# Units of up to 288 tokens with stationary weights, beside slots of 128 tokens, in the expert stage of an attention, FFN and MoE kernel

## The chip, the cores and the metric

The kernel runs on one core of a Trainium2 chip. The metric is the device time of one execution in microseconds (us). The median of three runs of the kernel before is 658.79 us (658.10 to 659.89).

## The reference

Three layers follow each other on 4 batches of 576 positions, 2304 tokens of 512 numbers. First comes attention with 8 heads of 64 and a window of 64 positions. Then a gated FFN: `h = relu(x @ w_in)`, a 3-tap convolution of h along the sequence, `(h * sigmoid(conv)) @ w_out`. The last layer is the one that the change touches. It sends each token to one of 8 experts:

```python
for s in range(S):
    fresh_e = argmax(logits[b, s])
    e = fresh_e if s == 0 or local_gate[b, s] < 0.5 else prev_e
    p = softmax(logits[b, s])
    h = np.maximum(x[b, s] @ w1[e], 0.0)      # 512 -> 1024
    out[b, s] = p[e] * (h @ w2[e])            # 1024 -> 512
```

With the reference's inputs (seed 0) the experts 0 to 7 get 336, 124, 567, 401, 257, 532, 13 and 74 tokens. The kernel does not know these numbers beforehand: it computes the routing on the chip.

## The kernel before

Attention and FFN run interleaved, batch by batch. In the last batch TensorE also computes the logits, and the routing follows while TensorE still makes the last FFN outputs (`tail`, line L484 with 512 columns, L524 with 256). Those outputs go to a scratch tensor `y_dram`, one row per token. The block `with tc.manual_schedule(engines=...)` at the end of the function fixes the order of TensorE (PE), VectorE (DVE) and ScalarE (ACT) by hand: `ahead(n)` emits the next n FFN matmuls, `next(sl)` the next part of `slots_of`, `cast` and `rest_of` prepare the first weights.

`slots_of` cuts each expert's tokens into slots of 128. It makes 0/1 matrices: `A` (the place of a token in its slot) and `bm` (which slot, which token). 18 matmuls of `A` with `bm` (L882) turn them into `gidx`, the row of `y_dram` for each place of each slot, and `sidx`, where its result goes; places that no token fills get a row that is not written. `eslot` is a slot's expert, `echg` says whether it differs from the slot before. A second product (L919) gives `pslot`, the probability by which a result is scaled. Slot 0 is not gathered whole: its rows come from a gather of `y_dram` (L1180, tile x0) and from the last two FFN tiles, through matmuls with `ident` and `aZ` (L514).

`run` then treats slots one by one; 23 of at most 25 are unrolled, the other two stand under `tc.If`. For a slot t:

- `gather(t)` (L1041): 128 rows of 2 KB from `y_dram` into SBUF, issued by GpSimd (POOL).
- `X(t)`: four transposes on PE into `psX`, then ACT copies the rounded part `xh` and DVE the remainder `xl`.
- `MM1`: 24 matmuls of 512 columns (three products of high and low parts, four blocks of 128 inputs, two halves of the 1024 hidden numbers). The tokens are the stationary operand, the weights move. ACT applies relu (L1074).
- `HT`: eight transposes of h (L1085), again split into `hh` (ACT, L1087) and `hl` (DVE, L1088).
- `MM2`: 24 matmuls of 512 columns (L1100), ACT scales the result (L1105), POOL scatters 128 rows (L1106).
- weights: `load1`/`load2` on SyncE's (SP's) queue into `raw1`/`raw2` (2 MB each, in four pieces, skipped where `echg` is 0); `split` makes high parts (ACT, L1017) and low parts (DVE, L1022). Every slot is split anew, also where the expert stays. There are two sets of split weights for each of w1 and w2.

All of a slot's steps stand in one fixed order per engine; MM2 of slot t-1 stands behind MM1 of slot t, so that ACT and DVE have a whole matmul phase to finish `hh` and `hl`.

## Time and profile before

| | |
|---|---|
| median of 3 runs | 658.79 us |
| profiled execution | 659.42 us, span 657.4 us |
| TensorE busy | 630.4 us (96%) |
| VectorE busy | 500.2 us (76%) |
| ScalarE busy | 468.2 us (71%) |
| GpSimd busy | 122.3 us (19%) |
| slots computed | 23 (23 scatters, L1106) |

The span is what the profiler sees between the first and the last instruction; the execution's own time is 2.0 us longer. TensorE's matmuls overlap in the records: one of 512 columns is shown with 0.39 us, while the next one starts 0.23 us after it. So the distance between starts is read, not the duration.

### The profile page before, as it was taken

What the parts mean: (1) busy time and instruction counts of PE and PEld (TensorE: products, weight loads), DVE (VectorE), ACT (ScalarE), POOL (GpSimd) and SP (SyncE); (2) the same over time, 40 slices, a digit from 0 to 9 for tenths busy, and PEclk for the clock granted to TensorE, in tenths of its full rate; (3) what the DMA queues carried; (4) which work ended last, traced back from release to release, by engine and by line L of the source; (5) the groups of instructions that cost most, each with busy time, mean ns of one, the idle gap of its engine ahead of it and who ended that gap; (6) DMA issues with size and microseconds to landing.
All of it is one profiled execution on the core that took longest, in us unless ns stands there. A gap on an engine that the chain in (4) does not pass through costs nothing.

```text
span 657.4 us, 12963 instructions
## 1 busy us (share of the span) xinstructions
PE 630.4 (96%) x4422; PEld 551.4 (84%) x4422; DVE 500.2 (76%) x995; ACT 468.2 (71%) x991; POOL 122.3 (19%) x158
## 2 busy tenths in 40 slices
PE   6879899999999999999999999999999999999995
PEld 5658898999999999999868778888888888888883
DVE  3789999426782388627766798998998988988982
ACT  3577688547792588735624688888888888888881
POOL 3412000001330023233602212112112112111101
PEclk9889999999999999999999999999999999999998
DMA  7894433332334211144001157504333434503770
GB/s 184 196 241 116 110 93 94 95 101 54 70 77 110 65 38 34 49 166 171 2 33 64 35 207 268 176 32 129 137 111 118 139 120 162 170 33 102 241 253 13
DMA packets 90885, 75.77 MB, mean 115 GB/s; under 512 B 71266, under 2 KB 71282, under 8 KB 90816
## 3 DMA queue, kind: packets, MB, share of 16 engines
q1 hardware_dynamic: 85696, 62.80, 32.3%
q0 software_dynamic: 3776, 10.80, 4.9%
q10 hardware_dynamic: 1344, 1.31, 0.7%
q8 instruction: 36, 0.59, 0.4%
q14 instruction: 33, 0.27, 0.1%
HBM read 127.84 MB, written 11.27 MB: 212 GB/s over the span
## 4 chain that ended last, share of the span: by engine, by line
PE 36%; issue 32%; DMA 14%; DVE 11%; ACT 4%; POOL 2%; POOLq 0%; ACTq 0%; DVEq 0%
PE psO L484 14%; PE psM L442 11%; DMA out_dram<-h,sidx 10%; PE psA L219 2%; DMA raw<-in_moe_w_in_dram 2%; PE psA L296 2%; POOL xg L1041 1%; DVE lf L570 1%; PE psA L271 1%; DVE sS L256 1%; PE psA L186 1%; ACT sS L243 1%; DVE lf L572 1%; PE psG L553 1%; DVE sS L231 1%
## 5 line engine op out<-in xcount | busy, mean ns | idle before, releaser
L442 PE MATMUL psM<-x,winH 128*128 128x288 f32 x512 | 109.3, 303 | 0.0
L442 PEld LDWEIGHTS psM<-x,winH 128*128 128x128 f32 x512 | 82.0, 188 | 1.0
L471 POOL TENSOR_TENSOR gL<-h,gH 128x64 fp32r<-128x64 f32 (+5 forms) x46 | 44.3, 975 | 204.5 <-ACT gH L470 102.3
L442 PE MATMUL psM<-x,winL 128*128 128x288 f32 x256 | 75.3, 295 | 0.0
L484 PE MATMUL psO<-woutH,gH 128*128 128x262 f32 (+2 forms) x240 | 68.3, 314 | 1.3 <-ACT gH L470 1.0
L1022 DVE TENSOR_TENSOR gL<-raw,gH 128x1024 fp32r<-128x1024 f32 x56 | 65.6, 1220 | 2.2 <-ACT gH L1017 0.7
L1106 POOL DMA_INDIRECT out_dram<-h,sidx x23 | 23.4, 1016 | 233.3 <-ACT h L1105 228.5
L484 PE MATMUL psO<-woutL,gH 128*128 128x262 f32 (+2 forms) x240 | 66.2, 303 | 0.0
L484 PE MATMUL psO<-woutH,gL 128*128 128x262 f32 (+2 forms) x240 | 64.8, 300 | 0.0
L243 ACT ACTIVATE sS<-sS,mx 128x128 f32<-128x128 f32 (+1 forms) x144 | 55.1, 387 | 7.7 <-DVE mx L231 7.7
L1022 DVE TENSOR_TENSOR winL<-raw,winH 128x1024 fp32r<-128x1024 f32 x48 | 56.4, 1235 | 3.6 <-ACT winH L1017 3.6
L1017 ACT ACTIVATE gH<-raw 128x1024 fp32r<-128x1024 f32 x56 | 55.8, 1066 | 0.0
L1022 DVE TENSOR_TENSOR woutL<-raw,woutH 128x1024 fp32r<-128x1024 f32 x44 | 51.0, 1221 | 2.8 <-ACT woutH L1017 2.8
L442 PEld LDWEIGHTS psM<-x,winL 128*128 128x128 f32 x256 | 48.0, 188 | 0.1
L1017 ACT ACTIVATE winH<-raw 128x1024 fp32r<-128x1024 f32 x48 | 47.0, 1061 | 0.0
L1100 PE MATMUL psO<-x,hh 128*128 128x512 f32 x144 | 46.7, 404 | 0.0
L1022 DVE TENSOR_TENSOR x<-raw,x 128x1024 fp32r<-128x1024 f32 x36 | 42.0, 1220 | 5.2 <-ACT x L1017 4.2
L484 PEld LDWEIGHTS psO<-woutH,gH 128*128 128x128 f32 x240 | 42.4, 189 | 3.9 <-ACT gH L470 1.4
L1100 PE MATMUL psO<-gH,hh 128*128 128x512 f32 x112 | 44.6, 398 | 0.0
L1100 PE MATMUL psO<-gH,hl 128*128 128x512 f32 x112 | 44.0, 393 | 0.0
L484 PEld LDWEIGHTS psO<-woutL,gH 128*128 128x128 f32 x240 | 42.7, 189 | 1.2
L1100 PE MATMUL psO<-gL,hh 128*128 128x512 f32 x112 | 43.7, 391 | 0.0
(289 smaller groups left out, 1625.8 us busy)
## 6 DMA issues: line engine op xcount, KB each, us to landing
raw<-in_moe_w_dram SPq DMA_DIRECT2D x184, 512.0 KB
v<-in_v_dram SPq DMA_DIRECT2D x56, 128.0 KB
y_dram<-ysb SPq DMA_DIRECT2D x18, 256.0 KB
kt<-in_k_dram SPq DMA_DIRECT2D x32, 128.0 KB
raw<-in_moe_w_out_dram SPq DMA_DIRECT2D x8, 512.0 KB
qt<-in_q_dram SPq DMA_DIRECT2D x30, 128.0 KB
raw<-in_moe_w_in_dram SPq DMA_DIRECT2D x6, 512.0 KB
raw<-in_moe_w_in_dram ACTq DMA_DIRECT2D x2, 512.0 KB
```

The lines of the kernel that those rows point to most:

```text
L186: nc.tensor.transpose(ps[:, n * P:(n + 1) * P], src[:, n].rearrange("p h d -> p (h d)"), ident)
L219: nc.tensor.matmul(ps[:, j * P + lo:(j + 1) * P], qbd[:, c, :], kT[:, k0:W * (c + 1)], start=True, stop=True)
L231: nc.vector.tensor_tensor_reduce(sS[:, c, lo:P], ps[:, j * P + lo:(j + 1) * P], mask[:, lo:P], -scale, -NEG, op0=ALU.add, op1=ALU.min, acc ...
L243: nc.scalar.activation(sS[:, c, lo:P], sS[:, c, lo:P], AF.Exp, scale=-1.0, bias=mx[:, c:c + 1], accum_out=sume[:, c:c + 1],)
L296: nc.tensor.matmul(ps[64 * h:64 * h + 64, W * (c - c0):W * (c - c0) + W], vt[:, h, :], a[:, c % 3, 64 * h:64 * h + 64], start=True, stop=True,
L442: nc.tensor.matmul(ps[:, 0:HS], wt[:, kk, f * P:(f + 1) * P], xt[:, c0:c0 + HS], start=n == 0, stop=n == 3 * KD - 1,)
L471: e1.tensor_tensor(gL[:, f, r:r + m], t[:, done:done + m], gH[:, f, r:r + m].bitcast(F32), op=ALU.subtract)
L484: nc.tensor.matmul(p_[:, 0:cs.stop - cs.start], gt[:, kk, r:r + P], wt[:, kk, cs], start=n == 0, stop=n == 3 * KF - 1,)
L1017: nc.scalar.activation(H_, raws[kk], AF.Copy)
L1022: nc.vector.tensor_tensor(L_, raws[kk], H_.bitcast(F32), op=ALU.subtract)
L1100: nc.tensor.matmul(ps, a[:, kk], w[:, kk % 2, :], start=n == 0, stop=n == 3 * KF - 1)
L1106: nc.gpsimd.indirect_dma_start(out=out[:, :], out_offset=bass.IndirectOffsetOnAxis(ap=sidx[:, t:t + 1].bitcast(U32), axis=0), in_=o, in_of ...
```

## The change

`units` is a fixed list: slots (S) and big units (B) alternate, S B S B S B S B S B S, and then more slots, up to 15 slots and 5 big units. 14 units, 9 S and 5 B, are always run; the other six slots stand in `If`s within each other. `slots_of` gets a planner: which experts give a big unit (up to 256 tokens and up to 32 of the next slot, at most 5 in all), how many slots stay, and which column of `gidx`, `sidx` and `pslot` each original slot becomes. The tables are made transposed (`tabI`, `tabP`), copied to SBUF by ACT and permuted by small matmuls (`placed`).

In a big unit the weights are stationary and up to 288 tokens move: `first_B` has 8 groups of 12 matmuls of 288 columns and needs no transposes of h; `second_B` has 4 groups of 24, and its output is transposed back by `Y` (12 transposes) during the slot that follows. `X` has 12 transposes for a big unit. MM2 now stands directly behind MM1 of its own unit; there is one set of split w2 in place of two, and one buffer of x and of gathered rows. The splits are handed out as jobs between matmul groups. Cut to its core:

```diff
+        NB = 5
+        XB = 32
+        WB = 2 * P + XB
         TS = (N + E * (P - 1)) // P
-        TB = TS - 2
+        NS = TS - 2 * NB
+        units = [("S", 0)]
+        for i in range(NB):
+            units += [("B", i), ("S", i + 1)]
+        units += [("S", i) for i in range(NB + 1, NS)]
+        NU = 2 * NB + 4
...
+            def table(m, name):
+                ps = pst(m * TS, P)
+                for i in range(NT):
+                    nc.tensor.matmul(ps, bm[:, i, 0:m].rearrange("p c t -> p (c t)"), rt["A"][:, i, :], start=i == 0, stop=i == NT - 1)
+                nc.scalar.activation(rt[name][:, 0:P], ps, AF.Copy)
+                return rt[name]
+
+            ti = table(2, "tabI")
...
+            def placed(t, c):
+                n = t.shape[0]
+                ps = pst(P, NCOL)
+                nc.tensor.matmul(ps[:, 0:CX], t[:, 0:P], perm[0:n, c], start=True, stop=True)
+                for j in range(3):
+                    nc.tensor.matmul(ps[:, CX:NCOL], t[:, j * XB:j * XB + P], permx[0:n, c, j], start=j == 0, stop=j == 2)
+                return ps
+
+            ps_i = placed(ti, 0)
+            v.tensor_scalar(gidx, ps_i, -float(P), 0.0, op0=ALU.add, op1=ALU.max)
...
+    def X(t):
+        xh, xl = xT_
+        for j, (_, u, n) in enumerate(cols(t)):
+            ps = psx() if j < 2 else psy().rearrange("p (k x) -> p k x", x=P)
+            for kk in range(KD):
+                nc.tensor.transpose(ps[:, kk, 0:n], xg[j][0:n, kk * P:(kk + 1) * P], ident[0:n, 0:n])
+            nc.scalar.activation(xh[:, :, u:u + n], ps[:, :, 0:n], AF.Copy)
+            nc.vector.tensor_tensor(xl[:, :, u:u + n], ps[:, :, 0:n], xh[:, :, u:u + n].bitcast(F32), op=ALU.subtract)
...
+    def Y(t, j):
+
+        c, u, n = cols(t)[j]
+        ps = psy()
+        for d in range(KD):
+            nc.tensor.transpose(ps[0:n, d * P:(d + 1) * P], yT_v[:, d, u:u + n], ident)
+        nc.scalar.activation(o_v[j][0:n], ps[0:n], AF.Copy, scale=pslot[0:n, c:c + 1])
+        scatter(c, n, o_v[j])
...
+    def first_B(t, after):
...
+        for f in range(KF):
+            ps = ps_h.tile([P, DM], F32, tag="h", name="psH")[:, 0:WB]
+            n = 0
+            for kk in range(KD):
+                H_, L_ = (w[:, f * P:(f + 1) * P] for w in ws[kk])
+                xh, xl = x[kk]
+                for a, w in ((H_, xh), (H_, xl), (L_, xh)):
+                    nc.tensor.matmul(ps, a, w, start=n == 0, stop=n == 3 * KD - 1)
+                    n += 1
+            nc.scalar.activation(hh[:, f], ps, AF.Relu)
+            nc.vector.scalar_tensor_tensor(hl[:, f], ps, 0.0, hh[:, f].bitcast(F32), op0=ALU.max, op1=ALU.subtract)
+            after(f)
...
+        def ahead():
+            if not end:
+                X(t + 1)
+                if t + 2 < NU:
+                    gather(t + 2)
+
+        if kind == "S":
+            y = [lambda j=j: Y(t - 1, j) for j in range(3)] if before else [lambda: None] * 3
+            job(2)
+            first_S(t, {
+                (0, 6): (y[0], job), (0, 10): (y[1],),
+                (1, 4): (job, lambda: HT(0),), (1, 6): (y[2],), (1, 10): (lambda: job(9),),
+            })
+            ahead()
+            jobs.extend(second)
+            second_S(t, {3: (lambda: HT(1), lambda: job(9))})
+        else:
+            first_B(t, lambda f: job())
+            job(9)
+            ahead()
+            jobs.extend(second)
+            second_B(t, lambda d: job(2))
+            job(9)
...
+            if t == 0:
+                step(t, (), w1_jobs(1))
+            elif units[t][0] == "B":
+                step(t, w1_jobs(t + 1) + w2_jobs(t), w1_jobs(t + 2))
+            else:
+                step(t, w2_jobs(t), w1_jobs(t + 2) if t > 2 * NB - 1 else ())
```

A job of `w1_jobs(t)` or `w2_jobs(t)` is one cast on ACT and one subtraction on DVE; the last of four also emits the load of the next unit's weights.

What stands on PE around the first routing product, in the kernel before (psR<-bm,A is the product, psO an FFN output):

```order
L484 MATMUL psO<-woutL,gH 128x512
L484 MATMUL psO<-woutH,gL 128x512
L484 MATMUL psO<-woutH,gH 128x512
L882 LDWEIGHTS A
L882 MATMUL psR<-bm,A 128x50
```

and in the kernel after, where the product is followed by 24 FFN matmuls and then by `placed` (L1011, L1013):

```order
L926 LDWEIGHTS bm
L926 MATMUL psR<-A,bm 50x128
L484 MATMUL psO<-woutH,gH 128x512
L484 MATMUL psO<-woutL,gH 128x512
L484 MATMUL psO<-woutH,gL 128x512
...
L1011 LDWEIGHTS tabI
L1011 MATMUL psR<-perm,tabI 128x25
L1013 LDWEIGHTS tabI
L1013 MATMUL psR<-permx,tabI 128x5
L484 MATMUL psO<-woutH,gH 128x512
```

The first product stands 16 FFN matmuls earlier than before, and PE has a second place at which it needs DVE's result (`perm`, `permx`).

What stands on ACT through a slot of the kernel before (casts of w2, relu of MM1, x of the next slot, casts of w1, the result):

```order
L1087 ACTIVATE hh<-psX 128x512 x2
L1017 ACTIVATE x<-raw_0_3859 128x1024
L1017 ACTIVATE x<-raw_1_3860 128x1024
L1017 ACTIVATE x<-raw_2_3861 128x1024
L1017 ACTIVATE gH<-raw_3_3862 128x1024
L1074 ACTIVATE h<-psH 128x512 x2
L1055 ACTIVATE xh<-psX 128x512
```

and through the first half of a slot behind a big unit of the kernel after (L1264 the outputs of `second_B`, L1126 casts, L1201 the results of `Y`, L1219 relu, L1192 `HT`):

```order
L1264 ACTIVATE h<-psO 128x288 x2
L1126 ACTIVATE x<-raw_0_3859 128x1024
L1126 ACTIVATE x<-raw_1_3860 128x1024
L1201 ACTIVATE o_4822<-psY,pslot 128x512
L1126 ACTIVATE x<-raw_2_3861 128x1024
L1201 ACTIVATE o_4823<-psY,pslot 128x512
L1219 ACTIVATE h<-psH 128x512
L1126 ACTIVATE gH<-raw_3_3862 128x1024
L1192 ACTIVATE gH<-psX 128x4x128
```

Before the first relu of the slot ACT now has the last output of the big unit, three casts and two results of `Y`; the transposes of h follow in the middle of the slot's own first phase.

DVE in a big unit of the kernel after takes turns between the low part of a group's relu (L1236) and that of a weight piece (L1130):

```order
L1236 SCALAR_TENSOR_TENSOR gL<-psH,gH 128x288
L1130 TENSOR_TENSOR winL<-raw_0_3855,winH 128x1024
L1236 SCALAR_TENSOR_TENSOR gL<-psH,gH 128x288
L1130 TENSOR_TENSOR winL<-raw_1_3856,winH 128x1024
L1236 SCALAR_TENSOR_TENSOR gL<-psH,gH 128x288
```

There was no such turn before: DVE split weights in blocks of four.

## Rows read from the trace of the kernel before

**Rows 1.** Busy time by stretch: us, then PE, PEld, DVE, ACT, POOL, PEclk, DMA share, GB/s
```profile
362.35:648.84 286.49, 286.24 (x1376) 234.60 (x1376) 253.05 (x248) 240.83 (x313) 47.31 (x44) 1.00 0.41 140
604.00:612.40 8.40, 8.40 (x44) 6.89 (x44) 7.64 (x9) 6.69 (x10) 2.04 (x2) 1.00 0.87 304
```

**Rows 2.** Timeline of POOL, first and last of 19 scatters: start us, us, what
```profile
407.79 1.02 POOL L1106 DMA_INDIRECT out_dram<-h,sidx  x1 [10.10 <-ACT h L1105]
...
631.53 1.00 POOL L1106 DMA_INDIRECT out_dram<-h,sidx  x1 [11.46 <-ACT h L1105]
```

**Rows 3.** Timeline of PE, from a slot's last matmul to the next slot
```profile
567.90 0.39 PE L1100 MATMUL psO<-gH,hl 128*128 128x512 f32 x1
568.13 1.03 PE L1085 MATMUL psX<-ident,h 128*128 128x128 f32 x8
568.92 0.48 PE L1070 MATMUL psH<-woutH,xh 128*128 128x512 f32 x1
```

**Rows 4.** Timeline of PE, 12 FFN matmuls of 288 columns: first, and next group
```profile
310.06 0.43 PE L442 MATMUL psM<-x,winH 128*128 128x288 f32 x2
...
311.65 0.45 PE L553 MATMUL psG<-gH,woutH 128*10 128x256 f32 x2
```

**Rows 5.** Groups by line, 290 to 330 us: count | busy us, mean ns | idle
```profile
L442 PEld LDWEIGHTS psM<-x,winH 128*128 128x128 f32 x113 | 18.2, 188 | 0.6
L449 ACT ACTIVATE h<-psM 128x288 f32<-128x288 f32 x16 | 6.4, 398 | 3.1 <-PE psM L442 3.1
```

**Rows 6.** Groups by line, expert stage
```profile
L1022 DVE TENSOR_TENSOR gL<-raw,gH 128x1024 fp32r<-128x1024 f32 x56 | 65.6, 1220 | 2.2 <-ACT gH L1017 0.7
L1017 ACT ACTIVATE gH<-raw 128x1024 fp32r<-128x1024 f32 x56 | 55.8, 1066 | 0.0
L1088 DVE TENSOR_TENSOR hl<-psX,hh 128x512 fp32r<-128x512 f32 x46 | 29.8, 686 | 12.3 <-ACT hh L1087 12.3
L1105 ACT ACTIVATE h<-psO,pslot 128x512 f32<-128x512 f32 x22 | 15.2, 692 | 27.0 <-issue 25.8 <-PE psO L1100 1.2
```

**Rows 7.** Timeline of DVE and POOL in the routing
```profile
342.70 0.16 DVE L860 SCALAR_TENSOR_TENSOR ni<-psR,nmin 128x8 int32<-128x8 f32 x1
342.89 0.17 DVE L861 TENSOR_SCALAR ni<-ni 128x8 int32<-128x8 int32 x1
...
345.81 0.33 DVE L878 TENSOR_SCALAR bm<-sl,pcol 128x450 bf16<-128x450 bf16 x1
...
350.32 0.18 DVE L887 TENSOR_SCALAR gidx<-inv 128x25 int32<-128x25 f32 x1
350.41 0.17 DVE L889 TENSOR_SCALAR pad<-inv 128x25 f32<-128x25 f32 x1
...
350.79 1.13 POOL L1180 DMA_INDIRECT x<-y_dram,gidx  x1 [22.73 <-DVE pad L889]
350.92 0.48 DVE L894 TENSOR_SCALAR aZ<-A,z 128x128 f32<-128x128 bf16 x2
```

**Rows 8.** Timeline of PE in the same stretch
```profile
345.48 0.39 PE L484 MATMUL psO<-woutH,gH 128*128 128x512 f32 x1
...
349.22 0.63 PE L882 MATMUL psR<-bm,A 128*128 128x50 bf16 x18
...
356.46 0.38 PE L514 MATMUL psX<-ident,x 128*128 128x128 f32 x2
```

**Rows 9.** Busy time by stretch, around an idle PE early on
```profile
41.10:43.60 2.50, 0.03 (x1) 0.00 (x0) 2.43 (x12) 0.96 (x6) 0.06 (x1) 1.00 0.98 305
43.60:51.10 7.50, 6.97 (x58) 5.38 (x59) 5.67 (x16) 6.16 (x22) 0.06 (x1) 0.55 0.90 193
```

**Rows 10.** The first slot: PE and POOL timeline
```profile
362.35 0.50 PE L1070 MATMUL psH<-winH,x 128*128 128x512 f32 x1 [0.43 <-DVE pslot L920]
...
362.93 1.43 POOL L1041 DMA_INDIRECT xg<-y_dram,gidx  x1 [6.20 <-ACT gH L1017]
364.67 1.90 POOL L1041 DMA_INDIRECT xg<-y_dram,gidx  x1 [0.30 <-issue]
```

**Rows 11.** Line L1041's gathers, time from issue to landing
```profile
DMA to landing us min/median/max: 3.3/3.8/8.0
```

More of the change, by code (lines that the diff above doesn't have):

```diff
@@ L916, in slots_of @@
             yield
-            ps_p = pst(P, 3, TS)
-            for i in range(NT):
-                nc.tensor.matmul(ps_p, rt["A"][:, i, :], bp[:, :, i], start=i == 0, stop=i == NT - 1)
-            nc.vector.tensor_reduce(pslot, ps_p.rearrange("p c t -> p t c"), axis=AX.X, op=ALU.add)
+            tp = table(3, "tabP")
+            yield
+            v.tensor_copy(pslot, placed(tp, 1))
         def mix(main, side, share):
@@ L999, in load1, with load2 @@
             )
-    def load2(t, dst=None):
+    def load2(t, always=False):
         for kk in KORD:
@@ new lines, in X @@
+        for j, (_, u, n) in enumerate(cols(t)):
[4 more added lines that the diff above has]
+            nc.vector.tensor_tensor(xl[:, :, u:u + n], ps[:, :, 0:n], xh[:, :, u:u + n].bitcast(F32), op=ALU.subtract)
+        w = P if units[t][0] == "S" else WB
@@ new lines, in second_S, with second_B @@
+                for m in mids.get(n, ()):
+                    m()
+        c = cols(t)[0][0]
+        nc.scalar.activation(o_v[0], ps, AF.Copy, scale=pslot[:, c:c + 1])
+        scatter(c, P, o_v[0])
+    def second_B(t, after):
+        hh, hl = hT
+        for d in range(KD):
+            ps = ps_o.tile([P, DM], F32, tag="o", name="psO")[:, 0:WB]
+            n = 0
+            for f in range(KF):
+                H_, L_ = (w[:, f % 2, d * P:(d + 1) * P] for w in w2_set[f // 2])
+                for a, w in ((H_, hh), (H_, hl), (L_, hh)):
+                    nc.tensor.matmul(ps, a, w[:, f], start=n == 0, stop=n == 3 * KF - 1)
+                    n += 1
+            nc.scalar.activation(yT_v[:, d], ps, AF.Copy)
+            after(d)
@@ new lines, in step, with job @@
+    def step(t, first=(), second=()):
+        kind = units[t][0]
+        end = t + 1 == NU
+        before = t and units[t - 1][0] == "B"
+        jobs = list(first)
+        def job(n=1):
+            for _ in range(n):
+                if jobs:
+                    jobs.pop(0)()
+        def ahead():
[3 more added lines that the diff above has]
+                    gather(t + 2)
+        if kind == "S":
+            y = [lambda j=j: Y(t - 1, j) for j in range(3)] if before else [lambda: None] * 3
[14 more added lines that the diff above has]
+            job(9)
@@ L1171, in tail, with alone @@
+    def alone(t):
+        load1(t, True)
+        load2(t, True)
+        gather(t)
+        X(t)
+        for kk in KORD:
+            split1(t, kk)
+            split2(kk)
+        first_S(t)
+        HT(0)
+        HT(1)
+        second_S(t)
     def tail():
@@ L1206 @@
         next(sl)
-        for kk in KORD:
-            ahead(9)
-            cast(raw1, w1s, "a", 0, kk)
-        ahead(2)
+        w1c = [lambda kk=kk: cast(raw1, w1_sets[0], kk) for kk in KORD]
+        ahead(11)
+        w1c.pop(0)()
+        ahead(11)
+        w1c.pop(0)()
+        next(sl)
+        ahead(12)
+        w1c.pop(0)()
+        ahead(12)
+        w1c.pop(0)()
         next(sl)
@@ L1213 @@
         for kk in KORD[0:3]:
-            cast(raw2, w2s, "b", 0, kk)
+            cast(raw2, w2_set, kk)
         for kk in KORD[0:3]:
-            rest_of(raw1, w1s, 0, kk)
-        ahead(14)
-        rest_of(raw1, w1s, 0, KORD[3])
+            rest_of(raw1, w1_sets[0], kk)
+        ahead(9)
+        next(sl)
+        ahead(4)
+        rest_of(raw1, w1_sets[0], KORD[3])
         for _ in rest:
```

415 lines of the change are left out of this document (224 added, 191 removed).

## The prediction

> **What bounds the kernel now.** I read the busy times by stretch first, then the timeline of one slot, then the groups by line, then the routing before the first slot. In the expert stage, first matmul to last, PE is busy for 286.2 of 286.5 us at the full granted clock; DVE has 253 us, ACT 241 us, the DMA engines 41% [rows 1]. PE is the bound, DVE is close behind. The profile agrees with the code: 19 scatters are 223.74 us apart, so a slot takes 223.74/18 = 12.43 us, and 23 slots make 285.9 us [rows 2]. Within a slot eight transposes take 0.79 us, 0.1 each [rows 3]; with the four of X that is 1.2 us, and the 48 matmuls of 512 columns take 11.23 us, 0.234 each. In the FFN, 12 matmuls of 288 columns, each with its own weights, take 1.59 us, 0.1325 each [rows 4]. By columns 288/512 of 0.234 would be 0.132: the pace goes by columns, whichever operand is stationary.
>
> **The work of PE.** The trace has 23 slots. The reference's inputs give tokens per expert of 336, 124, 567, 401, 257, 532, 13, 74; by the planner's rules that is 5 big units (experts 2, 2, 3, 4, 5) and 9 slots (0, 0, 0, 1, 3, 5, 5, 6, 7), exactly the 14 units that always run, so no `If` is taken. A slot: 48 x 0.234 + 8 x 0.1 = 12.03 us, nine are 108.3. A big unit: 192 x 0.1325 = 25.44 us, five are 127.2. X: 8 slots x 4 + 5 units x 12 = 92 transposes, 9.2 us; Y: 60, 6.0 us. The sum is 250.7 us against 285.9: 35.2 us less. The gain is padding alone: a big unit costs what 2.25 slots' matmuls cost (25.3 us), but 9 + 5 x 2.25 = 20.25 slots are left of 23.
>
> A rule speaks against this. The rows show 0.234 and 0.1325 us, in proportion to the columns. The Trainium skill, "TensorE: Matmul & The Clock Gate", section "Back-to-back issue gap", gives a stream of weight loads and matmuls about 81 ns at 128 columns and 131 ns at 512, so wide matmuls would be cheap per column. On a line between the two, 288 columns are about 100 ns (an estimate of mine from that page of the Trainium skill), and a big unit would be dearer than the slots it replaces by a third. The trace does not agree with its 131 ns, and the sum goes by the rows.
>
> **What comes onto the path in the units.** I follow ACT, which is in order, with the mean durations of its groups [rows 5, 6]: a cast 1.07 (counted as 1.0 where casts follow each other), a result or relu of 512 columns at most 0.69, one of 288 columns 0.40.
> - Slot behind a big unit. From the end of the big unit ACT does its last output (0.15 + 0.4), two casts (to about 2.65), result Y0 (3.3), a third cast (4.3), result Y1 (5.0), and only then relu of the first half (5.6). PE reaches the transposes of that h after 16 matmuls and 8 transposes of Y, 16 x 0.234 + 0.8 = 4.5 us. It waits about 1.1 us; 0 if ACT is quicker throughout, 1.9 with full durations and gaps. Five slots: 5.5 us.
> - Slot behind a slot. ACT: result 0.7, three casts (3.9), relu (4.5); PE is there after 3.7 us. About 0.7 us, three times: 2.1 us.
> - First half of a big unit. DVE alternates a 1.22 us subtraction with a 288-column low part, whose price is not in the trace: the nearest rows are 0.69 for 512 columns from PSUM on DVE and 0.40 for 288 on ACT [rows 5, 6]; I take 0.45. That is 1.6 to 1.67 us per group, and PE makes a group in 1.59. With two PSUM buffers PE falls behind by about 0.5 us over eight groups (0 with 0.37; 1.3 with 0.53). Five units: 2.5 us.
> - First unit. Its successor needs three gathers. Before, two gathers issued 0.6 and 2.3 us after the first matmul, taking 1.43 and 1.90 us of POOL [rows 10], and one lands 3.3 to 8.0 us after its issue [rows 11]. A third starts near 4.5 us and lands near 8.3; PE wants its rows after 24 matmuls and four transposes, 6.0 us. About 2.2 us once (0 to 6).
> - Hidden: the splits themselves (14 of each kind in place of 23; DVE has room), the scatters (POOL is mostly idle), and the loads. Expert changes after the first unit rise from 7 to 11, 4.2 MB each. The tightest is w1 of the unit after next: its four pieces go out as the splits of the first half free `raw1`, 4.5 to 9.5 us into a big unit, and are cast from 17 us on, one group later each. One set of 2.1 MB fits into 8.4 us at 304 GB/s [rows 1]. SP's queue holds them in the order in which they come free, so none waits behind a later one.
> These sum to 12.3 us.
>
> **Before the first unit.** DVE starts the slot planning at 342.70 and ends `bm` at 346.14 [rows 7]; the changed chain has three small instructions more (0.1 to 0.2 each), so about 346.45. PE now wants `bm` 16 matmuls earlier, at 345.48 instead of 349.22 [rows 8]: it waits 1 us. The transposed product has 128 columns instead of 50: about 1.1 us, in place of 0.6. PE then makes 24 matmuls and is at `placed` at about 353.1. DVE meanwhile does `aZ` (to 347.05) and 47 instructions until `perm`. Dependent ones follow at 0.2 us (342.70, 342.89), independent ones at 0.1 (350.32, 350.41) [rows 7]; 32 and 15 of them, plus 0.9 us for the longer ones and `perm`, make 8.8 us: 355.9. PE waits 2.8 us (4.5 if all took 0.21, none if all took 0.1). Of such small instructions the rows show 0.16 us busy and 0.2 us from start to start. The Trainium skill's table in "VectorE: DVE Perf Modes", section "The TRN2 errata — SBUF-src ops pay a fixed extra latency per instruction", gives 58 cycles plus one per element, about 69 ns here at its 0.96 GHz; by it this wait would be gone and the time some 4 us lower. The trace shows twice to three times that.
>
> Then `gidx` is there at 356.4, the gather of x0 goes out at 356.9 and lands near 360.7 (3.8 us; up to 364.9); PE has 3 matmuls of 512 and 34 of 256 columns before it needs it, 4.8 us: 361.0, no wait at the median. From there to the first matmul it was 362.35 - 356.46 = 5.9 us [rows 8, 10]. To it come ACT's copy of `tabP`, four small matmuls and a longer product, in a row: 1.8 us. The first unit starts at 368.7, 6.4 us later than before.
>
> One more: after PE had been idle for 2.5 us early in the kernel, the granted clock averaged 0.55 for 7.5 us, half speed (1.2 GHz) for most of them [rows 9]. The 2.8 us wait is of that size. I expect a drop here, shorter since dense work follows, and partly hidden under the gather: +1.2 us (0 to 3.4, half of 6.8). So 7.6 us before the units. The extra iotas on POOL lie where it idles; I count them as nothing, at most 1 us.
>
> **Sum.** 659.42 - 35.2 + 12.3 + 7.6 = 644.1 us for an execution like the profiled one; the median of the runs is 0.6 us lower, so 643.5 us. What follows the last matmul (8.6 us of the span) stays.
>
> **The rivals.**
> - *ACT and DVE keep pace.* The waits in the units are worked out from mean durations and overlap by little; if PE never waits in them, 12.3 us are saved: 631.2 us. For it: DVE and ACT lose about 40% of the splits. Against it: the order on ACT puts three casts and two results ahead of the relu.
> - *Waits in every slot lower the clock.* The place is the transposes of h in a slot behind a big unit. If that wait is not 1.1 but 2.5 us, as in rows 9, half speed follows for some 7 us: 1.4 + 3.5 = 4.9 us in each of five slots, 24.5 in all: 668 us, slower. It decides from a wait of that size on. Against it: four matmuls and the transposes of Y stand in between, PE is never quiet for long.
> - *Weights come late.* With `raw1` single, each big unit's second w1 has 12 us from issue to cast. A lateness of 3 us per big unit would eat 15 us and end at 658.5, no change; 5 us gives 668. It begins where 2.1 MB take over 12 us, 175 GB/s; rows 1 show 304.
> - *Weight loads set the pace of 288 columns.* A load is 188 ns long [rows 5]. If each matmul waited for its own, a big unit would take 36.1 us and the time would be 697 us. The FFN has the same pattern and does not wait [rows 4]. The rule of the Trainium skill above would make big units dearer in the same way.
>
> **How the numbers follow.** My forecast 0.55, with 637 to 651 as its own range; no waits in the units 0.25 (626 to 637); the lower clock 0.08, late weights 0.09 (650 to 675 each, a third of it within or below no change), the pace of weight loads 0.03. What this kernel's timing can tell from no change is about 0.3%, 2 us. The range of 8 in 10 is 628 to 655. Faster 0.86, same 0.03, slower 0.11.
>
> **What would show it.** In the profile after: 288-column groups of PE at 1.59 us per 12; the stage from first to last matmul at about 264 us; PE waiting for ACT's relu at the transposes of h, about 1 us, in slots behind big units; two waits for DVE before the first unit, 1 and 3 us, and a dip of the clock behind them; the first unit at about 369 to 370 us. Wrong would be a stage of PE without waits, casts waiting for DMA, or a clock below full within the units.

## The result, and the profile after

The changed kernel takes 649.45 us (median of four; 647.62 to 650.53) against 658.93 us for the kernel before: ratio 0.9853, 95% interval 0.9824 to 0.9882. It is faster, inside the range forecast (628 to 655), but 6 us above the forecast of 643.5. The profiled execution is the fastest of the four: 647.62 us, with a span of 645.9; the prediction's sum for such an execution was 644.1. Its miss of 3.5 us is made up of pieces of both signs, the larger ones of about that size:

| part (profiled executions) | before | after, forecast | after, measured | miss |
|---|---|---|---|---|
| start of the first unit | 362.35 | 368.7, +1.2 for the clock | 367.75 | -2.2 |
| first to last matmul of the stage | 286.49 | 22.9 less: 263.6 | 266.97 | +3.4 |
| last matmul to the end of the span | 8.56 | 8.6 | 11.18 | +2.6 |
| outside the span | 2.02 | 2.02 | 1.72 | -0.3 |

The stage by stretch, which answers to [rows 1] (columns as there): first the whole stage, then units 2 to 11 alone, and two stretches in the first unit and one in the routing.

```profile
367.75:634.72 266.97, 258.73 (x1616) 230.58 (x1616) 168.38 (x189) 168.43 (x247) 51.85 (x46) 0.99 0.60 206
388.17:595.73 207.56, 205.41 (x1373) 188.49 (x1372) 132.48 (x153) 135.72 (x202) 42.68 (x38) 1.00 0.62 210
352.00:358.00 6.00, 4.37 (x28) 3.58 (x27) 5.46 (x32) 2.95 (x4) 1.71 (x2) 1.00 0.02 4
...
376.00:378.00 2.00, 0.00 (x0) 0.00 (x0) 0.00 (x0) 0.00 (x0) 0.00 (x0) 0.55 1.03 397
378.00:380.00 2.00, 1.20 (x6) 1.20 (x7) 0.00 (x0) 0.05 (x1) 0.00 (x0) 0.50 0.17 61
```

Before, PE stood still for 0.25 us of the stage; now for 8.2 us, of which only 2.2 us lie in the ten units of the second line; the prediction counted 8.0 us of waits there (five slots at 1.1, five big units at 0.5). DVE and ACT each fell to 168 us. PE is still the bound. The 288-column matmuls keep the FFN's pace [rows 4]; the timeline of PE at the start of the second unit shows twelve of them in 1.59 us:

```profile
388.17 0.30 PE L1233 MATMUL psH<-gH,woutH 128*128 128x288 f32 x1
...
389.76 0.40 PE L1233 MATMUL psH<-gH,woutL 128*128 128x288 f32 x1
```

From first matmul to first matmul the 14 units take, in us: slot 20.42; big 26.86; slot 15.40; big 26.19; slot 15.40; big 26.18; slot 15.39; big 26.16; slot 15.41; big 26.17; slots 14.40, 13.15, 13.12, and 12.72 to the last matmul. The prediction's terms give 15.4 for the first, 26.3 for a big unit, 15.5 for a slot behind one and 13.1 for a slot behind a slot. Only the first is far off, by 5 us. (That the others fit although the waits do not is taken up in the account of the prediction.)

**The routing.** The timeline of PE between the FFN's matmuls and the first unit, answering to [rows 8, 10] (in brackets the idle time before an instruction and what ended it):

```profile
346.83 1.19 PE L926 MATMUL psR<-A,bm 128*50 128x128 bf16 x18 [0.80 <-DVE bm L916]
...
355.42 0.17 PE L1011 MATMUL psR<-perm,tabI 50*128 50x25 bf16 x1 [1.63 <-DVE perm L1002]
...
366.93 0.19 PE L1011 MATMUL psR<-perm,tabP 75*128 75x25 bf16 x1 [0.37 <-ACT tabP L927]
...
367.75 0.50 PE L1215 MATMUL psH<-winH,x 128*128 128x512 f32 x1 [0.57 <-DVE pslot L1033]
```

The two waits forecast at 1 and 2.8 us are 0.80 and 1.63. The second did not lower the clock in this execution: 1.00 from 352 to 358 us. In others it did. Ten traces have this wait, of 1.61 to 1.65 us (the changed kernel and runs 1 to 8 and 10 below, in which nothing moves it); in five of them (runs 1, 3, 6, 8 and 10) the clock was at 0.50 for 3.4 us right behind it, as in run 6:

```profile
354.66 0.17 PE L1011 MATMUL psR<-perm,tabI 50*128 50x25 bf16 x1 [1.62 <-DVE perm L1002]
355.00:358.60 3.60, 3.60 (x15) 3.30 (x16) 3.45 (x7) 0.60 (x1) 3.03 (x3) 0.53 0.33 92
```

From the first table matmul (L926) to the first unit these five take 22.2 to 22.3 us, the other five 20.8 to 21.0. So such a drop costs 1.3 us, and the profiled execution is one without it.

**The first unit.** The timelines of SP, POOL and PE, in order of time, answering to [rows 10]:

```profile
361.71 2.61 SPq L1107 DMA_DIRECT2D raw<-in_moe_w_dram  x3
...
364.41 0.38 SPq L531 DMA_DIRECT2D y_dram<-ysb  x1
...
368.86 3.78 SPq L1117 DMA_DIRECT2D raw<-in_moe_w_dram  x4
...
371.36 1.80 POOL L1159 DMA_INDIRECT xg<-y_dram,gidx  x1 [10.76 <-PE psH L1215]
...
373.47 1.00 POOL L1159 DMA_INDIRECT xg<-y_dram,gidx  x1 [0.30 <-issue]
...
374.77 0.93 POOL L1159 DMA_INDIRECT xg<-y_dram,gidx  x1 [0.30 <-issue]
...
378.80 1.97 PE L1179 MATMUL psX<-ident,xg 128*128 128x128 f32 x8 [4.74 <-DMA xg<-y_dram,gidx]
```

Before, the first gather started 0.6 us behind the first unit's first matmul; now 3.6 us behind, though its indices are there from 356 us on, and PE waits 4.74 us for the rows. Here the clock falls: 0.55 and 0.50 in the table above, back at 1.00 from about 383 us. The engine named as releaser (PE, L1215) is only the event that came last. A gather reads `y_dram`, and the last store to it (L531) is issued right behind three 512 KB pieces of weights. The trace has the times at which a transfer's semaphore counts up: the store's last count comes at 370.51, 6.1 us after its issue, and POOL gets past its wait for this semaphore at 370.54. In the kernel before, the same store landed 2.0 us after its issue (360.09 to 362.10). It too stood behind three pieces on SP's queue, but they moved nothing: slot 1 there has the expert of slot 0, so they were skipped, and the DMA engines were all but idle. SP's timeline and the busy times of a stretch in the kernel before, and then a stretch of the changed one:

```profile
355.96 3.09 SPq L995 DMA_DIRECT2D raw<-in_moe_w_dram  x3
360.09 0.34 SPq L531 DMA_DIRECT2D y_dram<-ysb  x1
355.00:360.00 5.00, 5.00 (x44) 4.89 (x42) 5.00 (x5) 1.09 (x3) 1.73 (x1) 1.00 0.01 3
```
```profile
362.00:366.00 4.00, 3.97 (x40) 3.78 (x39) 3.42 (x4) 0.77 (x2) 0.00 (x0) 1.00 0.80 246
```

Whether the weights make the store late, and what makes the gathers slow, is the question of the first experiments.

**The end.** Timelines of PE, ACT and POOL behind the last matmul, and POOL's sequencer at the `If` line (durations in ns, min/median/max):

```profile
634.72 0.40 PE L1246 MATMUL psO<-gH,gL 128*128 128x512 f32 x1
...
635.48 0.69 ACT L1251 ACTIVATE o<-psO,pslot 128x512 f32<-128x512 f32 x1 [4.60 <-PE psO L1246]
...
636.44 0.98 POOL L1166 DMA_INDIRECT out_dram<-o,sidx  x1 [12.25 <-ACT o L1251]
```
```profile
L1415 POOLq EVENT_SEMAPHORE  x4: 17/43/2323, 637.0 to 639.5; - x4
...
L1415 POOLq INC_SWDGE_SEM  x1: 1220/1220/1220, 639.6 to 639.6; - x1
```

POOL waits 2.3 us at the branch not taken before its closing work begins. In the kernel before, the same instruction's longest wait is 43 ns.

### The profile page after: what moved, and what is told of

It is laid out like the page before. It is cut to its first block, busy times and chain, and to the rows that moved or that the text cites. A ratio compares the mean times of both kernels' runs of the same rounds, so it can differ in the third digit from the quotient of the medians.

```text
span 645.9 us, 12841 instructions
## 1 busy us (share of the span) xinstructions
PE 601.4 (93%) x4670; PEld 545.5 (84%) x4670; DVE 424.2 (66%) x980; ACT 396.2 (61%) x927; POOL 128.1 (20%) x179
## 4 chain that ended last, share of the span: by engine, by line
PE 60%; DVE 13%; ACT 9%; DMA 8%; issue 7%; POOL 0%; SPq 0%; ACTq 0%; POOLq 0%; DVEq 0%
PE psO L484 12%; PE psM L442 11%; PE psO L1262 10%; PE psH L1233 9%; PE psO L1246 4%; PE psA L219 2%; DMA xg<-y_dram,gidx 2%; ACT x L1126 2%; PE psA L296 2%; ACT sS L243 2%; DMA raw<-in_moe_w_in_dram 2%; DVE lf L570 1%; PE psA L271 1%; DVE lf L572 1%; PE psH L1215 1%
## 5 line engine op out<-in xcount | busy, mean ns | idle before, releaser
L1130 DVE TENSOR_TENSOR x<-raw,x 128x1024 fp32r<-128x1024 f32 x42 | 50.3, 1224 | 27.3 <-ACT x L1126 26.4
L1166 POOL DMA_INDIRECT out_dram<-o,sidx x24 | 26.6, 1108 | 141.0 <-ACT o L1201 63.3
L1262 PE MATMUL psO<-gH,x 128*128 128x288 f32 x240 | 51.2, 297 | 0.0
L1233 PE MATMUL psH<-gH,woutH 128*128 128x288 f32 x160 | 48.3, 302 | 0.2 <-DVE gL L1236 0.2
L1233 PE MATMUL psH<-gH,woutL 128*128 128x288 f32 x160 | 47.3, 296 | 0.0
L1233 PE MATMUL psH<-gL,woutH 128*128 128x288 f32 x160 | 47.2, 295 | 0.0
L484 PEld LDWEIGHTS psO<-woutH,gL 128*128 128x128 f32 x240 | 42.4, 189 | 1.2
L1126 ACT ACTIVATE x<-raw 128x1024 fp32r<-128x1024 f32 x42 | 43.0, 1056 | 0.0
L1159 POOL DMA_INDIRECT xg<-y_dram,gidx x23 | 26.2, 1141 | 83.0 <-PE psX L1179 67.7
L1130 DVE TENSOR_TENSOR woutL<-raw,woutH 128x1024 fp32r<-128x1024 f32 x28 | 32.9, 1222 | 13.4 <-ACT woutH L1126 13.4
L1262 PEld LDWEIGHTS psO<-gH,x 128*128 128x128 f32 x240 | 39.3, 188 | 0.0
```

The costliest lines, as they stand in the source:

```text
L484: nc.tensor.matmul(p_[:, 0:cs.stop - cs.start], gt[:, kk, r:r + P], wt[:, kk, cs], start=n == 0, stop=n == 3 * KF - 1,)
L1126: nc.scalar.activation(dst[kk][0], raws[kk], AF.Copy)
L1130: nc.vector.tensor_tensor(L_, raws[kk], H_.bitcast(F32), op=ALU.subtract)
L1159: nc.gpsimd.indirect_dma_start(out=xg[j][0:n], out_offset=None, in_=y_dram[:, :], in_offset=bass.IndirectOffsetOnAxis(ap=gidx[0:n, c:c + 1 ...
L1166: nc.gpsimd.indirect_dma_start(out=out[:, :], out_offset=bass.IndirectOffsetOnAxis(ap=sidx[0:n, c:c + 1].bitcast(U32), axis=0), in_=o[0:n] ...
L1233: nc.tensor.matmul(ps, a, w, start=n == 0, stop=n == 3 * KD - 1)
```

## The experiments

Times of single runs scatter by 2 to 3 us (in kernels that are alike up to there the first unit starts between 367.3 and 369.9 us and lasts 20.4 to 21.8 us), so parts are compared inside the trace: the length of a unit, or a gap between two instructions.

**1. The last store of y from ACT's queue.**

```
-            nc.sync.dma_start(out=y_dram[...], in_=ysb)     # ffn_out_last
+            nc.scalar.dma_start(out=y_dram[...], in_=ysb)
```

> The last store of y is issued by ACT instead of SP, nothing else. Theory A (the gathers of the first big unit start late because the last store of y stands on SP's queue behind three of the four 512 KB pieces of the next unit's first weights, issued from 361.7 us): the store starts some 1 us earlier and shares the engines with those pieces instead of queuing behind all of them, the first gather of the big unit starts at 367 to 369 us instead of 371.4, and the first unit lasts 16.5 to 18.5 us instead of 20.4. Rival B (the gather waits until the memory of its tiles is released by TensorE, the reason that the wait list names last): gather still at 371 us, first unit 20.4 us. Time of the kernel by A: 2 to 4 us less than the changed kernel's; by B: the same.

648.95 us; the gather starts at 372.36, 3.4 us behind the first matmul, and the unit lasts 21.39. That looks like rival B, but the premise failed: ACT issued the store at 365.58, 0.1 us behind the issue of the fourth piece (at 365.46), not ahead of them.

```profile
361.59 4.21 SPq L1107 DMA_DIRECT2D raw<-in_moe_w_dram  x4
...
365.58 0.34 ACTq L531 DMA_DIRECT2D y_dram<-ysb  x1
```

From another queue the small transfer did not pass the large ones already issued: the store landed and POOL's first wait ended at 371.5, 5.9 us after the store's issue (6.1 in the changed kernel). Open until the fifth run.

**2. The second weights later.** `load2(1)` was written behind the gathers and transposes in the program.

> The four 512 KB pieces of the first big unit's second weights are issued behind its gathers and transposes instead of at 368.9 us; nothing else. Theory C (these pieces slow the gathers on the DMA engines: 7.4 us from the start of the first gather to its landing, against 3.3 to 4.3 elsewhere): the gathers start at 371 us as before but the first lands by 375.5 instead of 378.8, TensorE waits about 1 to 1.5 us for it instead of 4.7, the clock does not fall, and the first unit lasts 15.5 to 17 us instead of 20.4. Rival D (three gathers of 1 to 1.8 us each on POOL, one behind the other, set the landing): the wait stays above 4 us, the first unit above 19.5 us. By C the kernel is 3.5 to 5 us faster than the changed one.

647.98 us, first unit 21.53. The pieces still went out at 368.82 us:

```profile
368.82 3.83 SPq L1117 DMA_DIRECT2D raw<-in_moe_w_dram  x4
```

SP issued them as soon as their buffers were free, whatever their place in the program, so this was the changed kernel once more. It tells nothing of theory C, and is a repeat for the scatter above.

**3 and 4. The end.**

```
-        if t < len(units):          # e4: two further slots kept
+        if t < NU + 2:
```
```
-    others(NU)                      # e5: one branch, six bodies
+    with tc.If(slots > units[NU][1]):
+        for t in range(NU, len(units)):
+            alone(t)
```

> Only two of the six further slots behind the last unit are kept (the other four, which run only for other inputs, are left out): two nested branches, as in the kernel before. Theory E (the branch that is not taken ends by waiting for every DMA semaphore that its body uses; six bodies use all eight of POOL's, the one of the last scatter among them, so that POOL waits 2.3 us for this scatter before it begins its end work of 1.2 + 4.2 us): from the last matmul's start to the end of the span 8.5 to 9.0 us instead of 11.2, and POOL's wait at the branch gone. Rival F (the end is late for another reason: the last scatter itself, or TensorE's jump of 3.5 us over a long body): by the scatter 11.2 us; by the jump a shorter jump and between the two.

> One branch around all six further slots instead of six nested branches. If the number of DMA semaphores in the body decides (theory E), the end stays at about 11 us from the last matmul and POOL's wait of 2.3 us at the branch stays. If the depth of the branches decides (each with its own end code), the end falls to 8.5 to 9 us.

With two further slots the time is 646.36 us and the end takes 8.8 us; with six bodies in one branch 649.61 us and 11.2. POOL's sequencer at the branch in the two:

```profile
L1415 POOLq EVENT_SEMAPHORE  x2: 17/30/43, 638.2 to 638.2; - x2
```
```profile
L1413 POOLq EVENT_SEMAPHORE  x4: 17/42/2325, 638.9 to 641.4; - x4
```

So the 2.3 us come from how much stands inside the branch, not from its depth; TensorE's jump (0.36 us long in the first, 3.44 in the second) is over 3.5 us before POOL's wait ends. What POOL waits for can be read from the numbers of the semaphores in the traces. Six bodies use POOL's DMAs twelve times and two use them four times. With six, POOL waits at the branch for eight semaphores, and the long wait is for two of them, one of which the last scatter counts up: that one's last count comes at 639.42 us in the changed kernel and the wait ends at 639.45, 3.0 us after the scatter's start. With two bodies POOL waits for four, and the last scatter's is not among them. Theory E holds.

**5 and 6. The store ahead of the weights; the second weights from ACT.**

```
-    with tc.manual_schedule(engines={..PE, ..DVE, ..Activation}):
+    with tc.manual_schedule(engines={..PE, ..DVE, ..Activation, ..SP}):
```
```
-        load2(1)                                    # in run(); second run only
+                if t == 0:                          # in step(0), behind X(1)
+                    load2(1, eng=nc.scalar)
```

> SP keeps the written order in the routing stage, so that the last store of y is issued ahead of the four pieces of the first big unit's first weights; the same work otherwise. Theory A (the store lands late because it is queued behind three 512 KB pieces, 6 us from its issue to the end of POOL's wait): the store lands within 3 us, the first gather starts by 368.5 us, within 1 us of the first unit's first matmul (in the changed kernel 3.6 us behind it), and the first unit lasts 16 to 18.5 us instead of 20.4. Rival B (the memory of the gathers' tiles, released by TensorE): the gather still starts about 3.5 us behind the first unit's first matmul and the unit lasts 20 to 22 us.

> As the one before, and the second weights of the first big unit are issued by ACT behind that unit's transposes instead of by SP as soon as their buffers are free. Theory C (these pieces slow the gathers): the gathers land 3 to 4.5 us from their issue, TensorE's wait for them is under 1.5 us, the granted clock stays at 1.00 and the first unit lasts 15 to 16 us, 4.5 to 6 us less than in the changed kernel; the weights themselves land by 385 us, before they are needed in the big unit. Rival D (three gathers in a row on POOL set the landing): no more gain than from the order of the store alone.

The first took 642.95 us. SP and POOL in it:

```profile
363.16 0.32 SPq L531 DMA_DIRECT2D y_dram<-ysb  x1
365.23 2.38 SPq L1107 DMA_DIRECT2D raw<-in_moe_w_dram  x4
```
```profile
365.93 1.05 POOL L1159 DMA_INDIRECT xg<-y_dram,gidx  x1 [6.40 <-ACT x L1146]
```

Theory A holds: with the store in front (the pieces now follow it, 3.5 us later than before) it lands 2.0 us after its issue, the gather starts 0.6 us ahead of the first matmul, and the first unit lasts 16.42 us. Rival B falls. What is left are waits of 0.65 and 1.78 us, since the gathers still need 7.4 to 8.5 us to land.

The second took 646.65 us, first unit 17.92. Its second weights went out at 379.85, but the three gathers landed 7.0, 8.0 and 6.6 us after their starts all the same. Holding back the second weights alone, as theory C has it, gains nothing: the 2 MB of first weights issued at 367.00 to 369.4 were now beside the gathers. (In the changed kernel the first weights had landed by 371.8 us, and it was the second that ran beside them.) Rival D was not yet excluded. That this run took 3.7 us longer than run 5 is mostly the clock: it fell behind the wait for perm, as shown above, and again for 3.4 us at 379 us. The second unit took 27.82 us, 1.1 more than in run 5.

**7. Casts behind the first transposes of h.**

```
-                (0, 6): (y[0], job), (0, 10): (y[1],),
-                (1, 4): (job, lambda: HT(0),), (1, 6): (y[2],), ...
+                (0, 6): (y[0],), (0, 10): (y[1],),
+                (1, 4): (lambda: HT(0),), (1, 6): (job, y[2]), ...
```

> In the slots the third and fourth cast of the second weights are handed out behind the first four transposes of h instead of ahead of them. Theory G (ACT's relu of the first half stands behind these casts, and TensorE's first transpose of h waits 1.1 to 1.3 us for it): slots behind a big unit fall from 15.40 to 14.2 to 14.7 us, slots behind a slot from 13.13 to 12.3 to 12.7, the sum of the stage by 5 to 8 us. Rival H (the casts are then late for the second product, which waits for its weights): the wait moves from the transposes to the second product, and the slots keep their length within 0.2 us.

649.61 us; slots behind a big unit rose from 15.40 to 15.66. The wait for the relu went (of PE's weight loads, over these units, 4.1 us before and 1.5 now), but it came back at the second transposes, behind DVE's work, which the moved casts had made late:

```profile
467.30 0.65 PE L1189 MATMUL psX<-ident,h 128*128 128x128 f32 x4 [0.59 <-DVE gL L1181]
```

Neither text fits whole: the wait moved on, as rival H has it, but to DVE's work and not to the weights, and these slots became 0.26 us longer, not shorter.

**8. 256 columns in the big units.** `[:, 0:WB]` became `[:, 0:256]` in both products; the up to 32 last tokens of each big unit are left out.

> The big units stream 256 columns instead of 288 (the up to 32 last tokens of each big unit are left out of both products; the transposes and scatters stay). By the rows of 288 columns (0.1325 us from start to start) and of 128-column work a matmul of 256 takes 0.113 to 0.118 us if its columns set the pace: 192 x 0.0145 to 0.019 = 2.8 to 3.7 us less for each of five big units, 26.17 to about 22.4 to 23.4 us, 14 to 18 us in the kernel. Rival (the weight load before each matmul sets the pace, or ACT and DVE do): the big units keep 26.2 us.

640.0 us; big units 24.32 us, 1.85 less. In the second product twelve matmuls took 1.43 us (0.119 each), by columns:

```profile
487.82 0.28 PE L1263 MATMUL psO<-gH,x 128*128 128x256 f32 x1
...
489.25 0.41 PE L1263 MATMUL psO<-gH,x 128*128 128x256 f32 x2
```

The second product fell from 12.77 to 11.63 us, the first only from 12.92 to 12.22: there PE now waits for DVE's low parts. Columns set the pace, the weight loads do not, and the first product has little room above DVE's pace. The expected 2.8 to 3.7 us per big unit were too many for that reason.

**9. The experts' tables behind perm.** The ten instructions (`ge` to `tcnt`) moved behind `permx`, SP's order as in run 5.

> SP in written order as in the run before (641.2 us span, first unit at 366.5), and the ten DVE instructions that fill SP's tables of experts for the units are put behind the two that give the tokens' places (perm, permx). Theory K (TensorE's wait of 1.6 us for perm, with some 1.8 us without a matmul, is the length of DVE's chain): perm comes 1.3 to 1.6 us earlier, TensorE waits at most 0.4 us there, the first unit starts 1.2 to 1.6 us earlier and the span falls to 639.5 to 640.2. Rival L (what sets the first unit's start is the gather for unit 0 or the table of gates further on): the wait goes, but the first unit starts at most 0.4 us earlier.

645.01 us; the first unit started at 366.45, as without the edit. PE's wait for perm fell to 0.32 us, and a new one stood further on:

```profile
353.08 0.17 PE L1010 MATMUL psR<-perm,tabI 50*128 50x25 bf16 x1 [0.32 <-DVE perm L983]
...
359.36 0.49 PE L514 MATMUL psX<-ident,x 128*128 128x128 f32 x2 [1.00 <-DMA x<-y_dram,gidx]
```

The moved group now stood ahead of `gidx` on DVE, so the gather for unit 0 went out no earlier. Rival L. In this run the waits in the first unit were 0.34 and 2.12 us, hardly more than in run 5, yet the clock fell to 0.50 from 375 us on and the unit lasted 19.22.

**10. Four big units.** `NB = 4`, 16 units.

> Four big units instead of five (12 slots and 4 big units do what 9 slots and 5 big units did; nothing else). Theory M (the change gains by padding alone, at the price per unit that the trace of the changed kernel shows): one big unit of 26.2 us and one slot behind a big unit of 15.4 us go, four slots of 13.1 us come, so the stage is 10.9 us longer: 277 to 279 us, kernel 657 to 660. Rival (the big units gain by something else, as fewer waits or fewer weight loads per token; then a slot more costs less or a big unit less gains more than its matmuls): a difference outside 9 to 13 us.

660.47 us; the stage takes 278.38 us, 11.4 more than the changed kernel's (10.8 without the first two units; 10.9 was expected). Theory M: the gain is padding, at the units' own prices.

**11. Parts together.** Runs 5 and 9, and the casts moved out of the crowded stretch:

```
-                (0, 6): (y[0], job), (0, 10): (y[1],),
-                (1, 4): (job, lambda: HT(0),), (1, 6): (y[2],), (1, 10): (lambda: job(9),),
+                (0, 6): (y[0],), (0, 10): (y[1],),
+                (1, 4): (lambda: HT(0), job,), (1, 6): (y[2],),
```

> The kernel with SP in written order and the tables of experts behind perm, and with the third cast of the second weights handed out behind the first transposes of h and the fourth behind the second transposes, in the second product, where ACT has little to do. Theory G' (ACT is full from the slot's start to its second transposes, some 8.9 us of 9.4; a cast moved within that stretch moves the wait, one moved out of it takes it away): slots behind a big unit 14.4 to 14.9 us instead of 15.4, slots behind a slot 12.5 to 12.9 instead of 13.1, 4 to 6 us in the stage; with the other two parts 634 to 639 us for the kernel, 0.964 to 0.970 of the kernel before. Rival H (the moved cast is late for the last weights of the second product): slots at 15.2 us or more, kernel 641 to 643.

640.05 us (639.36 to 641.45), ratio to the kernel before 0.9706, interval 0.9681 to 0.9731: below the changed kernel's interval, and the lowest median of the versions that compute everything. Slots behind a big unit take 14.87 us, slots behind a slot 12.50, so the units behind the first two take 4.6 us less together, as expected; the time expected with the other parts, 634 to 639 us, was missed. ACT in such a slot:

```profile
458.94 0.59 ACT L1218 ACTIVATE h<-psH 128x512 f32<-128x512 f32 x1
...
465.14 0.60 ACT L1191 ACTIVATE gH<-psX 128x512 fp32r<-128x512 f32 x1 [0.82 <-PE psX L1188]
465.64 1.05 ACT L1125 ACTIVATE gH<-raw 128x1024 fp32r<-128x1024 f32 x1
```

PE's matmuls no longer wait for the relu (2.0 us in units 2 to 11 before, now none); the last cast runs in the second product, where ACT is idle until 470. Theory G'. The first unit takes 19.39 us, with waits of 0.82 and 1.56 and the clock at 0.50, 3 us more than in run 5; the start gained nothing, as in run 9.

**12. First weights behind the gathers.**

```
+        slot_regs(1)
+        nc.sync.dma_start(out=mark[:, :], in_=xg[1][0:1, 0:16])
         load1(1)
```

and the tables' ten instructions behind `sidx`.

> The kernel of the last run (640.05 us) with two edits. One: the ten instructions of the experts' tables stand behind gidx and sidx instead of between perm and gidx, where they had moved TensorE's wait of 1.6 us for perm into a wait of 1.0 us for unit 0's gather; by theory K' (the gather's chain is late by just these instructions) that wait goes, and the first unit's first matmul comes 19.5 to 19.9 us behind the first table matmul (tabI) instead of 20.6. Two: SP copies 64 bytes of the second gathered tile to memory before it issues the first weights of the first big unit, so these 2 MB are issued only when that tile has landed. Theory C' (it is the first weights, too, that slow the gathers: 7.4 to 8.5 us from start to landing, with the second weights moved away still 6.8 and 8.0): the first two gathers land 3 to 4.5 us from their start, TensorE's waits of 0.7 and 1.8 us in front of the transposes go, the clock stays at 1.00 and the first unit lasts 14 to 15.5 us instead of 19.4; the weights land by 380 us and hold up the big unit by at most 1 us. Rival D (the gathers are slow by themselves): they land 7 us late as before, the weights are then late too and the first two units together are longer than 45.5 us. By C' 633 to 636.5 us, 0.960 to 0.965 of the kernel before; by D 640 us or more.

642.50 us (640.19 to 643.69), ratio 0.9727 (0.9700 to 0.9755). Both edits did for the first unit what their theories say, but the kernel was not faster (633 to 636.5 us was expected): the time came back one unit later. The first unit starts 19.64 us behind the table matmul (20.63 before), takes 13.58 us without a wait, and the gathers land as in [rows 11] at their best:

```profile
DMA to landing us min/median/max: 3.4/3.5/3.7
```

What theory C' says of the gathers holds, and rival D falls. But C' let the weights hold up the big unit by 1 us at most, and that unit takes 35.01 us. POOL, SP, ACT and PE:

```profile
369.32 2.45 SPq L1107 DMA_DIRECT2D raw<-in_moe_w_dram  x4
372.10 2.80 SPq L1117 DMA_DIRECT2D raw<-in_moe_w_dram  x4
376.99 18.89 SPq L1107 DMA_DIRECT2D raw<-in_moe_w_dram  x8
```
```profile
386.88 1.06 ACT L1126 ACTIVATE winH<-raw 128x1024 fp32r<-128x1024 f32 x1 [5.53 <-DMA raw<-in_moe_w_dram]
...
387.84 0.39 ACT L1235 ACTIVATE gH<-psH 128x288 fp32r<-128x288 f32 x1
```
```profile
389.61 0.61 PE L1233 MATMUL psH<-gH,woutH 128*128 128x288 f32 x1 [5.54 <-DVE gL L1236]
```
```profile
371.00:386.00 15.00, 12.30 (x72) 10.21 (x70) 7.54 (x9) 7.06 (x11) 2.33 (x2) 1.00 1.02 386
...
389.50:392.00 2.50, 2.39 (x10) 2.39 (x11) 2.50 (x4) 0.96 (x2) 0.00 (x0) 0.50 0.67 215
```

From 371 to 386 us the DMA engines are full at 386 GB/s. ACT's next cast waits 5.5 us for its weights, the relu stands behind it on ACT, and PE stands still until 389.6; then the clock is at half. Three sets of weights have to come in the first two units (6.3 MB, about 16 us at that rate), and the edit issues the first of them 5 us behind the first matmul (369.32 to 364.27 us), where run 11 issues it 1.3 us ahead. That these loads bound the two units fits; no run tries it by itself. First two units together: 47.28 us in the changed kernel, 43.2 in run 5, 45.55 in run 11, 48.59 here. The intervals of runs 11 and 12 overlap.

## Why the prediction was right, and where it was off

- *Padding (35.2 us less).* Right. Run 10 gives one big unit back and costs 10.8 us behind the first two units, run 8 shows that columns set the pace. The weight-load rival falls. The Trainium skill's "TensorE: Matmul & The Clock Gate", section "Back-to-back issue gap", has 131 ns at 512 columns; the trace of the changed kernel again shows 0.23 us there and 0.1325 at 288, so it does not agree.
- *Waits in the units: the cause was right, the fit of the sums partly luck.* Slots behind big units 15.40 for 15.5, slots behind a slot 13.13 for 13.1, big units 26.17 for 26.3. The cause in the slots, ACT's order, is shown by runs 7 and 11 together: moved by one place the wait only changes its name; moved to where ACT is idle, 0.5 to 0.6 us per slot go. But behind a big unit the wait was forecast at 1.1 us. Run 11, in which PE's matmuls wait for nothing there, still takes 14.87 us, where the terms without the wait give 14.4. So the wait was 0.5 us, and some 0.4 us are in the transposes, counted at 0.1 each: four of them put the next matmuls of 512 columns back by 0.45 us (run 11, 456.35 to 457.03 us, less one matmul of 0.23):

```profile
456.35 0.60 PE L1199 MATMUL psY<-ident,h 128*128 128x128 f32 x4
456.71 0.48 PE L1214 MATMUL psH<-winH,gH 128*128 128x512 f32 x1
457.03 0.40 PE L1214 MATMUL psH<-winL,gH 128*128 128x512 f32 x1
```

In the big units PE's matmuls waited for DVE by 0.2 us in all five together, where 0.5 us each was forecast, though DVE's low part has the price that was taken for it (0.452 us for 0.45); the 0.3 us by which such a unit is longer than its terms without a wait are not resolved. "ACT and DVE keep pace" was thus near the truth for DVE, and not the case for ACT.
- *First unit, 2.2 us for gathers: this step failed.* It cost 7 us: 4.74 of waiting and some 2 of half clock. I took the gathers' start and landing from [rows 10, 11] and only added a third. Neither is a property of the gathers alone. In the kernel before no weights moved in that stretch, since slot 1 has the expert of slot 0. Behind the change's first unit stands a big unit of another expert: its first weights go out just in front of the store of y for which the gathers wait (6.1 us instead of 2.0; run 5 puts this right: 4.0 us less in the unit, some 2 of them by the clock), and 2 MB of weights run beside the gathers, which then land 4.8 to 7.4 us after their starts (3.4 to 3.7 us in run 12, where no weights run beside them). The prediction counted four more changes of expert, but as hidden, and did not ask where the first of them falls. Its sentence that no load waits behind a later one was on weights alone; the store was left out of it.
- *Before the first unit, 7.6 us.* 5.4 measured in the profiled execution, by smaller waits (0.80 and 1.63 instead of 1.0 and 2.8) and no drop of the clock behind them. The missing drop is luck: five of ten traces have it, at 1.3 us each, which is the size that the prediction gave it (1.2). In the profiled execution the clock fell 20 us later, behind the 4.74 us wait. The two longest of the four executions have a lower mean clock (0.978 against 0.981 and 0.982), so that part of the median's 6 us may be this drop; no trace shows it. DVE's chain ended `perm` at 355.28 us, 355.9 was forecast. The table of the Trainium skill's "VectorE: DVE Perf Modes", section "The TRN2 errata — SBUF-src ops pay a fixed extra latency per instruction", by which this wait would have been gone, does not agree with the trace here. The same section says that this row gives too little, and that about 150 cycles were measured in place of its 58; that is about 0.16 us (an estimate from this page's 0.96 GHz), and with it the 0.16 us busy of [rows 7] agree.
- *What follows the last matmul stays: wrong by 2.6 us.* The prediction counted the `If`s as not taken, and gave them no time. Four more bodies inside the branch cost 2.3 us at the end (runs 3 and 4).
- *Weights come late.* Given 0.09, and not seen in the changed kernel, where ACT's casts wait 0.8 us in all for weights in units 2 to 11. Run 12 shows the mechanism, 8.9 us in one big unit, once the first unit is fast and its successor's weights are held back.
- *Lower clock in every slot.* Not seen: 1.00 throughout units 2 to 11. The size that it named for the wait, some 2.5 us, was no limit: in the five traces above the clock fell behind a wait of 1.6 us.

That the total lay only 6 us off owes something to misses of opposite sign: 5 us too little for the first unit and 2.6 for the end, 2.2 too much before the first unit and some 1.6 in the other units.

## What to carry to other kernels

When a change moves loads, list everything on that queue, small stores as well, and ask who waits for each: a 256 KB store behind 1.5 MB of weights held up a gather whose indices had long been ready. A start or a landing read from a trace is a price only under the traffic it was read in: the rows of before came from a stretch whose loads were skipped. When a wait is removed by moving an instruction, look at what then stands behind it; here the wait moved on three times (perm to the gather, first to second transposes, first to second unit), and went only where the instruction landed in a stretch in which its engine was idle. Code that does not run is not free if an engine has to wait for its resources on the way past it.

## What the runs showed of the hardware

- A store of 256 KB landed 2.0 us after its issue with no weights moving (kernel before, run 5) and 6.1 us behind three 512 KB pieces on the same queue (changed kernel). Issued on ACT's queue behind four pieces on SP's it landed no sooner: 5.9 us (run 1).
- Nearly the same pair of waits left the clock alone in one run and halved it in others: 0.65 and 1.78 us in run 5 (1.00 throughout), 0.34 and 2.12 in run 9, 0.82 and 1.56 in run 11 (0.50 for 6.8 us, about 3 us of time). Behind the wait of 1.6 us for perm it fell in five traces of ten (0.50 for 3.4 us, 1.3 us of time). What tips it was not settled.
- Three gathers landed in 3.4 to 3.7 us with 0.41 of the DMA engines' time in use (run 12, 366 to 371 us), and in 7.4 to 8.5 with 0.96 to 1.00 (run 5).
- A branch that is not taken made POOL wait 2.3 us, until the last scatter had landed, where its six bodies share that scatter's semaphore (changed kernel, run 4), and 0.04 us at most where its two bodies do not (run 3).
